# Fetching three attention weights already transposed by DMA, in place of turning them on TensorE, in a one-core recurrent-memory kernel

## The chip, the cores and the metric

The kernel runs on one core of one Trainium2 chip. The metric is the device time of one execution in microseconds (us). A separate execution, taken by the hardware profiler, gives the trace that is read here; its span is the time from the first to the last recorded instruction. PE is TensorE's matmul side and PEld its weight load, DVE is VectorE, ACT ScalarE, POOL GpSimd, SP the engine that issues most DMAs. L83 is line 83 of the kernel.

## The reference

Four layers follow one another on a bf16 tensor x of 2048 tokens by 448 features: attention with a recurrent memory, a gated feed-forward part, and both once more with the same weights. Cut to what matters:

```python
def attention(x, mem0, Wq, Wk, Wv, Wo, seg_len):        # 16 heads of 256, 8 memory rows
    mem = mem0
    for s in range(2048 // 32):
        h = concat([mem, x[32 * s:32 * s + 32]])        # 40 rows
        q, k, v = h @ Wq, h @ Wk, h @ Wv                # per head
        p = softmax(where(mask, q @ k.T * 256 ** -0.5, -1e9))
        o = (p @ v) summed over the heads through Wo
        mem = o[:8]                                     # feeds the next segment
        outs.append(o[8:])
x = x + attention(layernorm(x), ...)
x = x + (relu(n @ W_gate) * (n @ W_up)) @ W_down        # n = layernorm(x)
x = x + attention(layernorm(x), ...)
x = x + the same feed-forward part
```

Wq, Wk and Wv are 448 x 4096 each (16 heads of 256), Wo is 4096 x 448, all bf16: 3.67 MB each.

## The kernel before

The memory makes the 64 segments a chain. So the kernel does not form q, k and v per segment. It **fuses the weights first**: per head, A = Wq Wk^T (448 x 448) and B = Wv Wo (448 x 448), kept in SBUF as `A_sb` and `B_sb`. Then 69 steps (L747) follow, in which both attention layers run as two chains, the second `LAG` = 4 segments behind, and the feed-forward part of a block is fed in between (class `Feed`, L372).

The change touches only the fusing, L200 to L325, which comes ahead of the steps. TensorE contracts over the partitions of both operands, and A contracts over the head's 256 features, while Wq and Wk lie in memory with the 448 model features as rows. So each must be turned. The work goes in eight pairs of heads, p = 0 to 7, twice:

- **The q/k loop** (L272). `load_nat` (L215) brings 512 columns of a weight (two heads) in their natural layout into one of six tiles `nat` of 128 x 4 x 512: one DMA of 384 rows (L219, 384 KB), one of the last 64 rows (L220, 64 KB), and for Wq those 64 rows once more, into the other half of the partitions (L222). `flips` (L233) turns it: a `half` (L237) is eight 128 x 128 transposes on TensorE (`tr`, L85, tile `tpw`) and one copy of 128 x 1024 out of PSUM by DVE or ACT (L243). Two halves make one turned tile, `qT` or `kT`. Pair p's product is eight groups (kd, eo) of two matmuls of 384 columns (`aps`, L282) and two of 64 (`mxw`, L286), and copies into `A_sb` (L290 to L299).
- **The v loop** (L303). Pair p needs `vT`, turned likewise, and `wo`, 448 KB of Wo, fetched by POOL's queue (L308) into four buffers. Seven PSUM tiles `bps` of 448 columns are formed (L314 and L323) and copied into `B_sb`.

The turning is worked one pair ahead: `queue(p + 1)` (L247) gives the units of the next pair, and they are strewn between the groups of the present pair (L296, L317). TensorE's order is the program's order by hand: `in_order` (L74) chains every matmul and transpose to the one before. The other engines' instructions are ordered by the scheduler. `share` (L227) gives each copy out of PSUM to DVE or ACT, whichever has less by its table of costs. After p = 2 comes `first_rows` (L256): the normalised first 128 tokens are transposed on TensorE; their `rstd` is made on POOL (L161), behind POOL's memsets of L207 to L212.

PSUM tiles rotate through seven buffers. The tiles of the fusing lie in the pool `pre`, and the tiles of the steps (pool `main`, L334: `hk`, `Y1`, the feed-forward weights and others) are laid over it. The feed-forward weights come in pieces, each DMA tied to a point of TensorE's order (`next_piece`, L362).

Of the kernel before, what the change touches and what calls it, by code (L numbers as in the profile page):

```python
# [8 lines left out]
BF = mybir.dt.bfloat16  # L9
# [6 lines left out]
DM = 448  # L16
H = 16
NP = 8
# [36 lines left out]
def build_kernel(ctx, tc, A_x, A_mem0, A_Wq, A_Wk, A_Wv, A_Wo, B_W_gate, B_W_up, B_W_down, out,  # L55
                 ntiles=16, nseg=64):
    nc = tc.nc
    P = nc.NUM_PARTITIONS
# [4 lines left out]
    Wq = A_Wq.rearrange("d h e -> d (h e)")  # L63
    Wk = A_Wk.rearrange("d h e -> d (h e)")
    Wv = A_Wv.rearrange("d h e -> d (h e)")
# [3 lines left out]
    psum = ctx.enter_context(tc.tile_pool(name="psum", bufs=7, space=bass.MemoryType.PSUM))  # L69
# [4 lines left out]
    def in_order(r):  # L74
        if last_pe[0] is not None:
            tc.add_manual_dep(r.ins, last_pe[0],
                              mybir.DependencyInfo(mybir.DependencyClass.NoSync,
                                                   mybir.DependencyReason.DATA),
                              reason="order of issue")
        last_pe[0] = r.ins.name  # L80
# [4 lines left out]
    def tr(*a):  # L85
        in_order(nc.tensor.transpose(*a))  # L86
# [11 lines left out]
    def block(i):  # L98
        return slice(TB * i, TB * i + TB)
# [3 lines left out]
    ident = glob.tile([P, P], BF, name="ident")  # L103
# [19 lines left out]
    for b in range(4):  # L123
        o = 0 if b % 2 == 0 else MEM
# [8 lines left out]
    half = glob.tile([P, 1], F32, name="half")  # L133
# [6 lines left out]
    for i in range(2):  # L140
        t = glob.tile([P, BLK, HW], BF, name=f"hT{i}")
# [55 lines left out]
        nc.vector.tensor_copy(mem_of(g, cs)[:, 0:src.shape[1]], src)  # L197


    with tc.tile_pool(name="pre", bufs=6) as pre:  # L200
        mem0_n = pre.tile([MEM, 512], BF, name="mem0_n", bufs=1)
        nc.gpsimd.dma_start(mem0_n[:, 0:DM], mem0)
        nc.gpsimd.dma_start(mem0_n[:, DM:512], mem0[:, 384:DM])
        nats = []
        for i in range(6):
            t = pre.tile([P, 4, 512], BF, name=f"nat{i}", bufs=1)
            (nc.gpsimd if i % 2 else nc.vector).memset(t[64:128, 3, :], 0.0)  # L207
            nats.append(t)
        nc.gpsimd.memset(A_sb[64:128, 3, :, :, :], 0.0)
        nc.gpsimd.memset(A_sb[0:64, 3, 0, 0:4, :], 0.0)  # L210
        for t in TQ + TZ + PX + PM + YB:
            nc.gpsimd.memset(t[:], 0.0)  # L212
        nn = [0]

        def load_nat(src, p, eng):  # L215
            t = nats[nn[0] % 6]
            nn[0] += 1
            cols = slice(512 * p, 512 * (p + 1))
            eng.dma_start(t[:, 0:3, :], src[0:384, cols].rearrange("(k p) n -> p k n", p=P))  # L219
            eng.dma_start(t[0:64, 3, :], src[384:448, cols])  # L220
            if src is Wq:
                eng.dma_start(t[64:128, 3, :], src[384:448, cols])  # L222
            return t

        spent = {nc.vector: 0.0, nc.scalar: 0.0}

        def share(dst, src, n, per):  # L227
            cost = {nc.vector: 60 + n * per[0], nc.scalar: 170 + n * per[1]}
            eng = min(cost, key=lambda e: spent[e] + cost[e])
            spent[eng] += cost[eng]  # L230
            evac(eng, dst, src)

        def flips(src, p, name):  # L233
            nat = load_nat(src, p, nc.sync)
            o = pre.tile([P, 4, 512], BF, tag="tT", name=name)

            def half(e2):  # L237
                tp = psum.tile([P, 2, 512], BF, tag="ps", name="tpw")
                for e in range(2):
                    for kd in range(4):  # L240
                        tr(tp[:, e, kd * 128:(kd + 1) * 128],
                           nat[:, kd, (2 * e2 + e) * 128:(2 * e2 + e + 1) * 128], ident[:])
                share(o[:, 2 * e2:2 * e2 + 2, :], tp[:], 1024, (0.6, 0.82))  # L243

            return o, [lambda: half(0), lambda: half(1)]

        def queue(p):  # L247
            if p < NP:
                qT, a = flips(Wq, p, "qT")
                kT, b = flips(Wk, p, "kT")  # L250
                return (qT, kT), a + b
            if p == NP:
                return flips(Wv, 0, "vT")
            return None, []

        def first_rows():  # L256
            xn0 = normed(row_stats(xp[1]))
            if nblk > 3:
                nc.sync.dma_start(xp[1][0:TB, :], x_dram[block(3)])
            tps0 = transpose_tokens(xn0)  # L260
            for b in range(2):
                rows_in(nc.vector, b, 0, tps0[:, :, block(b)])
            mtp = psum.tile([P, 4, MEM], BF, tag="ps", name="mtp")
            for kd in range(4):
                tr(mtp[:, kd, :], mem0_n[:, kd * 128:(kd + 1) * 128], ident[0:MEM, 0:MEM])
            nc.vector.tensor_copy(mem0T[:], mtp[:])
            set_mem(0, mem0T[:].unsqueeze(2), (0,))

        ready, todo = queue(0)
        for u in todo:  # L270
            u()
        for p in range(NP):  # L272
            hf, p4 = divmod(p, 4)
            qT, kT = ready
            ready, todo = queue(p + 1)
            mx_ps = psum.tile([P, 4, 128], F32, tag="ps", name="mxw")
            for kd in range(4):
                for eo in range(2):
                    aps = psum.tile([P, 3, 128], F32, tag="ps", name="aps")
                    for t in range(2):  # L280
                        e = 2 * eo + t
                        mm(aps[:, :, :], qT[:, e, kd * 128:(kd + 1) * 128],  # L282
                           kT[:, e, 0:384], start=(t == 0), stop=(t == 1))
                    for t in range(2):
                        e = 2 * eo + t
                        mm(mx_ps[:, kd, eo * 64:eo * 64 + 64], qT[:, e, kd * 128:(kd + 1) * 128],  # L286
                           kT[:, e, 384:448], start=(t == 0), stop=(t == 1))
                    t0 = eo * 4 + p4
                    if kd < 3:
                        share(A_sb[:, kd, hf, t0:t0 + 17:8, :], aps[:], 384, (1.28, 0.85))  # L290
                    elif upper(hf, eo):
                        share(A_sb[64:128, 3, hf, t0, :], aps[64:128, 0, :], 128, (1.28, 0.85))
                        share(A_sb[0:64, 3, hf, t0 + 8:t0 + 17:8, :], aps[0:64, 1:3, :], 256, (1.28, 0.85))
                    else:
                        share(A_sb[0:64, 3, hf, t0:t0 + 17:8, :], aps[0:64], 384, (1.28, 0.85))
                    if todo and 2 * kd + eo in (0, 2, 4, 5):  # L296
                        todo.pop(0)()
            share(A_sb[:, 0:3, hf, 24 + p4, :], mx_ps[:, 0:3, :], 384, (1.28, 0.85))
            share(A_sb[0:64, 3, hf, 24 + p4, :], mx_ps[0:64, 3, :], 128, (1.28, 0.85))  # L299
            if p == 2:  # L300
                first_rows()

        for p in range(NP):  # L303
            hf, p4 = divmod(p, 4)
            vT = ready
            ready, todo = flips(Wv, p + 1, "vT") if p + 1 < NP else (None, [])
            wo = pre.tile([P, 4, DM], BF, tag="wo", name="wo", bufs=4)
            nc.gpsimd.dma_start(wo[:], Wo[:, 4 * p:4 * p + 4, :])  # L308
            for eo in range(2):
                for kd in range(3):  # L310
                    bps = psum.tile([P, 512], F32, tag="ps", name="bps")
                    for t in range(2):
                        e = 2 * eo + t
                        mm(bps[:, 0:DM], vT[:, e, kd * 128:(kd + 1) * 128], wo[:, e, :],  # L314
                           start=(t == 0), stop=(t == 1))
                    share(B_sb[:, hf, tidx(kd, eo, p4), 0:DM], bps[:, 0:DM], DM, (1.28, 0.85))
                    if kd == 1 and todo:  # L317
                        todo.pop(0)()
            bps = psum.tile([P, 512], F32, tag="ps", name="bps")
            for t in range(2):  # L320
                for eo in range(2):
                    e = 2 * eo + t
                    mm(bps[64 * eo:64 * eo + 64, 0:DM], vT[:, e, 384:448], wo[:, e, :],  # L323
                       start=(t == 0), stop=(t == 1), tile_position=(0, 64 * eo))
            share(B_sb[:, hf, 24 + p4, 0:DM], bps[:, 0:DM], DM, (1.28, 0.85))  # L325
# [12 lines left out]
    for i in range(2):  # L338
        t = main.tile([P, 5, 128], BF, name=f"hk{i}")
# [406 lines left out]
    pre = {}  # L746
    for g in range(nsteps + 1):  # L747
        if g == LAG - 1:
            set_mem(LAG, mem0T[:].unsqueeze(2), (1,))
        i = (g - 3) // 2  # L750
        pre = step(g, Feed(i) if g % 2 and 0 <= i < nblk + LAG // BLK - 1 else None, pre)
# [66 lines left out]
```

## Time and profile before

| what | value |
|---|---|
| three runs | 1678.39, 1678.39, 1681.45 us; median 1678.39 |
| the profiled execution's own time | 1679.21 us |
| its span | 1677.4 us (1.8 us lie around it) |
| granted TensorE clock, mean | 0.995 |
| PE busy over the span | 1630.9 us (97%), 41152 matmuls |
| DVE, ACT, POOL busy | 1184.3 (71%), 689.4 (41%), 87.8 us (5%) |
| HBM read | 23.70 MB |
| q/k loop, from its first product to the first `bps` | 9.0 to 47.5 us |
| v loop, to the first projection of the steps | 47.5 to 76.7 us |

Nearly the whole span is the 69 steps, with TensorE busy; the fusing is the first 76.7 us, 4.6% of it. Only that stretch holds the DMAs of Wq, Wk, Wv and Wo. Busy shares over the whole span say nothing of it, so it is read by stretches of its own.

### The profile page before, as it was taken

The numbers are of one execution on the slowest core, as the hardware profiler recorded it, in microseconds if no ns is written. First come the engines' busy times: TensorE is split into PE (matmuls) and PEld (weight loads), VectorE is DVE, ScalarE is ACT, GpSimd is POOL, SyncE is SP. The second block draws the span as 40 slices with busy tenths as digits, with TensorE's granted clock in tenths as the row PEclk, the third lists the DMA queues.
The fourth block names the chain that finished last, engine by engine and source line by source line (L and its number), as shares of the span: only waits on it lengthen the run. The fifth ranks groups of instructions, "written<-read, shape, count | busy, mean of one in ns | idle before, by whom it ended". The sixth has DMA issues, their size and how long they took to land.

```text
span 1677.4 us, 90576 instructions
## 1 busy us (share of the span) xinstructions
PE 1630.9 (97%) x41152; PEld 1523.0 (91%) x41152; DVE 1184.3 (71%) x4181; ACT 689.4 (41%) x2093; POOL 87.8 (5%) x178
## 2 busy tenths in 40 slices
PE   8999999999999999999999999999999999999997
PEld 6688999999999999999999999999999999999986
DVE  7766777777667767776677677766776777666774
ACT  6634443344333433443334334433344344333432
POOL 5200000000000000000000000000000000000000
PEclk9989999999999999999999999999999999999999
DMA  9430000000000000000000000000000000000000
GB/s 271 127 91 14 8 9 9 8 5 9 9 9 9 9 9 8 4 9 9 9 9 9 9 9 5 8 9 9 9 9 9 9 6 7 9 8 6 6 7 5
DMA packets 26785, 33.17 MB, mean 20 GB/s; under 512 B 3352, under 2 KB 24736, under 8 KB 26400
## 3 DMA queue, kind: packets, MB, share of 16 engines
q1 hardware_dynamic: 25312, 23.70, 5.0%
q8 instruction: 322, 5.28, 1.3%
q0 software_dynamic: 1088, 3.68, 0.7%
q14 instruction: 63, 0.52, 0.1%
HBM read 23.70 MB, written 1.84 MB: 15 GB/s over the span
## 4 chain that ended last, share of the span: by engine, by line
PE 84%; DVE 11%; ACT 2%; issue 1%; DMA 0%; POOL 0%; POOLq 0%; SPq 0%; DVEq 0%; ACTq 0%
PE prj L83 31%; PE ox L83 16%; PE ups L83 6%; PE gps L83 6%; PE dps L83 5%; PE o L83 5%; PE y L83 3%; PE Sx L83 2%; DVE Y L92 2%; DVE ssum L503 1%; PE bps L83 1%; PE tpw L86 1%; PE tps L86 1%; DVE mx L499 1%; PE aps L83 1%
## 5 line engine op out<-in xcount | busy, mean ns | idle before, releaser
L83 PE MATMUL prj<-hT,A_sb 128*128 128x80 bf16 (+3 forms) x15232 | 570.2, 199 | 1.0 <-issue 0.5
L83 PEld LDWEIGHTS <-A_sb 128*128 128x128 bf16 (+1 forms) x15232 | 544.0, 99 | 5.7 <-issue 1.6
L83 PEld LDWEIGHTS <-B_sb 128*128 128x128 bf16 (+1 forms) x15232 | 491.0, 103 | 17.5 <-issue 0.2
L83 PE MATMUL ox<-Y,B_sb 128*128 128x80 bf16 (+4 forms) x11424 | 438.7, 199 | 0.0
L90 ACT CAST TQ<-prj 128x320 bf16<-128x320 f32 (+1 forms) x456 | 170.0, 385 | 160.5 <-PE prj L83 128.2
L92 DVE CAST TQ<-prj 128x320 bf16<-128x320 f32 (+1 forms) x456 | 192.9, 430 | 44.6 <-PE prj L83 38.4
L90 ACT CAST Y<-y 128x512 bf16<-128x512 f32 (+2 forms) x384 | 145.7, 417 | 84.1 <-DVE Y L92 72.1
L92 DVE CAST Y<-y 128x128 bf16<-128x128 f32 (+2 forms) x384 | 161.4, 458 | 18.5 <-PE y L83 3.6
L83 PE MATMUL ups<-xT,Wu_sb 128*128 128x128 bf16 (+1 forms) x1904 | 140.6, 217 | 1.3 <-DVE xT L395 0.5
L83 PE MATMUL gps<-xT,Wg_sb 128*128 128x128 bf16 (+1 forms) x1904 | 140.5, 217 | 0.0
L83 PEld LDWEIGHTS <-hk 40*128 40x128 bf16 (+1 forms) x1950 | 102.2, 95 | 25.1 <-issue 10.9
L501 ACT ACTIVATE se<-se 128x80 f32<-128x80 f32 (+1 forms) x270 | 80.1, 303 | 102.2 <-DVE se L500 100.6
L635 ACT COPY os<-o 64x80 f32<-64x80 f32 (+3 forms) x68 | 14.9, 219 | 250.2 <-PE o L83 249.0
L408 ACT CAST ut<-ups 128x256 bf16<-128x256 f32 (+1 forms) x238 | 84.5, 355 | 69.5 <-PE ups L83 48.5
L83 PEld LDWEIGHTS <-Wg_sb 128*128 128x128 bf16 x1904 | 112.4, 99 | 0.7 <-issue 0.6
L409 DVE SCALAR_TENSOR_TENSOR hh<-gps,ut 128x256 bf16<-128x256 f32 (+1 forms) x238 | 93.1, 401 | 26.6 <-PE gps L83 15.3
L83 PEld LDWEIGHTS <-Wu_sb 128*128 128x128 bf16 x1904 | 110.7, 99 | 1.0 <-issue 1.0
L83 PE MATMUL dps<-Wd_sb,hh 128*128 128x448 bf16 x476 | 95.7, 353 | 0.0
L161 POOL TENSOR_SCALAR rstd<-mv 128x1 f32<-128x1 f32 x67 | 14.9, 223 | 1525.9 <-DVE mv L159 1476.4
L642 DVE TENSOR_TENSOR hT<-o,os 64x16 bf16<-64x16 f32 (+1 forms) x134 | 22.8, 170 | 98.3 <-ACT os L639 58.9
L418 DVE TENSOR_TENSOR xp<-dps,xa 64x448 bf16<-64x448 f32 x32 | 20.1, 627 | 95.2 <-PE dps L83 95.2
L90 ACT CAST TZ<-prj 64x320 bf16<-64x320 f32 (+2 forms) x152 | 56.1, 379 | 71.9 <-DVE TZ L92 68.8
(120 smaller groups left out, 2069.2 us busy)
## 6 DMA issues: line engine op xcount, KB each, us to landing
wo<-in_A_Wo_dram POOLq DMA_DIRECT2D x8, 448.0 KB, 5.4
nat<-in_A_Wq_dram SPq DMA_DIRECT2D x8, 384.0 KB, 5.5
nat<-in_A_Wk_dram SPq DMA_DIRECT2D x8, 384.0 KB, 4.9
nat<-in_A_Wv_dram SPq DMA_DIRECT2D x8, 384.0 KB, 4.6
xa<-in_A_x_dram SPq DMA_DIRECT2D x32, 56.0 KB, 2.2
xa<-xp SPq DMA_DIRECT2D x32, 56.0 KB, 1.9
out_dram<-xa SPq DMA_DIRECT2D x32, 56.0 KB, 2.0
xp<-in_A_x_dram SPq DMA_DIRECT2D x30, 56.0 KB, 2.1
```

Source lines behind the costliest of these rows:

```text
L83: in_order(nc.tensor.matmul(*a, **k))
L86: in_order(nc.tensor.transpose(*a))
L90: nc.scalar.copy(dst, src)
L92: eng.tensor_copy(dst, src)
L161: nc.gpsimd.tensor_scalar(out=rstd[:], in0=mv[:, 1:2], scalar1=EPS, scalar2=None, op0=ALU.add)
L408: nc.scalar.copy(ut[:, :, n], ups[:, :, n])
L409: nc.vector.scalar_tensor_tensor(out=hh[:, 2 * u:2 * u + 2, n], in0=gps[:, :, n], scalar=0.0, in1=ut[:, :, n], op0=ALU.max, op1=ALU.mult)
L418: nc.vector.tensor_tensor(self.nx[TB:P, :], dps[TB:P, 0:DM], self.x[TB:P, :], op=ALU.add)
L499: nc.vector.tensor_reduce(mx[:], Sp[:], axis=AX.X, op=ALU.max)
L501: nc.scalar.activation(se[:], se[:], AF.Exp, scale=SCALE)
L503: nc.vector.tensor_reduce(ssum[:], se[:], axis=AX.X, op=ALU.add)
L642: nc.vector.tensor_tensor(mem_of(g + 1, ms)[r, 3], o3[r, m0:m0 + nm].rearrange("p (c m) -> p c m", m=MEM), os[r, m0:m0 + nm].rearrange("p ...
```

## The change

Wq, Wk and Wv are no longer loaded in their natural layout. `flipped_in` asks the DMA to write 448 rows x 512 columns transposed: column n goes to partition n mod 128 of chunk n div 128, the rows lie beside one another. For Wq a second transposing DMA writes the last 64 rows once more behind them (columns 448 to 512 of the tile). The natural tiles, their memsets, the TensorE transposes and the copies out of PSUM go. Three pairs of qT and kT are asked for ahead of the loop, then pair p + 3 at the start of pair p; from p = 5 on, two tiles of vT in place of a pair. The pool `pre` has 12 turned tiles in place of 6 (and six natural ones less: the same space).

```diff
-    with tc.tile_pool(name="pre", bufs=6) as pre:
+    with tc.tile_pool(name="pre", bufs=12) as pre:
...
-        nats = []
-        for i in range(6):
-            t = pre.tile([P, 4, 512], BF, name=f"nat{i}", bufs=1)
-            (nc.gpsimd if i % 2 else nc.vector).memset(t[64:128, 3, :], 0.0)
-            nats.append(t)
...
-        def flips(src, p, name):
-            nat = load_nat(src, p, nc.sync)
+        def flipped_in(src, p, name):
             o = pre.tile([P, 4, 512], BF, tag="tT", name=name)
-
-            def half(e2):
-                tp = psum.tile([P, 2, 512], BF, tag="ps", name="tpw")
-                for e in range(2):
-                    for kd in range(4):
-                        tr(tp[:, e, kd * 128:(kd + 1) * 128],
-                           nat[:, kd, (2 * e2 + e) * 128:(2 * e2 + e + 1) * 128], ident[:])
-                share(o[:, 2 * e2:2 * e2 + 2, :], tp[:], 1024, (0.6, 0.82))
...
+            nc.sync.dma_start_transpose(o[:, :, 0:DM], src[:, 512 * p:512 * (p + 1)])
+            if src is Wq:
+                nc.sync.dma_start_transpose(o[:, :, DM:512], src[384:DM, 512 * p:512 * (p + 1)])
+            return o
...
-        ready, todo = queue(0)
-        for u in todo:
-            u()
+        turned = [(flipped_in(Wq, p, "qT"), flipped_in(Wk, p, "kT")) for p in range(3)]
         for p in range(NP):
             hf, p4 = divmod(p, 4)
-            qT, kT = ready
-            ready, todo = queue(p + 1)
+            qT, kT = turned.pop(0)
+            if p + 3 < NP:
+                turned.append((flipped_in(Wq, p + 3, "qT"), flipped_in(Wk, p + 3, "kT")))
+            else:
+                turned += [flipped_in(Wv, 2 * (p + 3 - NP) + i, "vT") for i in range(2)]
...
-                    if todo and 2 * kd + eo in (0, 2, 4, 5):
-                        todo.pop(0)()
...
-            vT = ready
-            ready, todo = flips(Wv, p + 1, "vT") if p + 1 < NP else (None, [])
+            vT = turned.pop(0)
+            if p + 6 < NP:
+                turned.append(flipped_in(Wv, p + 6, "vT"))
...
-                    if kd == 1 and todo:
-                        todo.pop(0)()
```

On the queues: SP issues 32 transposing DMAs (16 for Wq, 8 for Wk, 8 for Wv) where it issued 56 loads. The first eight DMAs of SP go out with no wait but for SP itself, from then on each waits for the one eight before it; the transposing ones of pair 6 and later wait for TensorE to be done with the tile twelve before. The reload of `xp` (L259 before), which waits for DVE's normalised rows, stands between the last two DMAs of Wq, and the loads of `xa` stand behind all of Wv.

More of the change, by code (lines that the diff above doesn't have):

```diff
@@ L212, in build_kernel @@
             nc.gpsimd.memset(t[:], 0.0)
[L213 to L223, printed above, removed]
         spent = {nc.vector: 0.0, nc.scalar: 0.0}
@@ L231, in share @@
             evac(eng, dst, src)
-        def flips(src, p, name):
-            nat = load_nat(src, p, nc.sync)
+        def flipped_in(src, p, name):
             o = pre.tile([P, 4, 512], BF, tag="tT", name=name)
-            def half(e2):
-                tp = psum.tile([P, 2, 512], BF, tag="ps", name="tpw")
-                for e in range(2):
-                    for kd in range(4):
-                        tr(tp[:, e, kd * 128:(kd + 1) * 128],
-                           nat[:, kd, (2 * e2 + e) * 128:(2 * e2 + e + 1) * 128], ident[:])
-                share(o[:, 2 * e2:2 * e2 + 2, :], tp[:], 1024, (0.6, 0.82))
[L245 to L254, printed above, removed]
+            nc.sync.dma_start_transpose(o[:, :, 0:DM], src[:, 512 * p:512 * (p + 1)])
+            if src is Wq:
+                nc.sync.dma_start_transpose(o[:, :, DM:512], src[384:DM, 512 * p:512 * (p + 1)])
+            return o
         def first_rows():
```

## The prediction

> **What bounds the kernel now.** I read the page's engine totals first (PE 97% of the span), then the busy time by stretch around the code that changes, then that stretch's instructions by form, the chain that ended last, and the DMA queues by window. The stretches, with busy us (count) of PE, PEld, DVE, ACT, POOL, then granted clock, DMA share and GB/s:
>
> ```profile
> 5.30:9.00 3.70, 3.40 (x32) 2.89 (x33) 1.44 (x3) 1.26 (x2) 3.70 (x3) 1.00 0.93 285
> 9.00:24.10 15.10, 15.08 (x201) 11.84 (x201) 12.58 (x24) 10.96 (x23) 15.02 (x18) 1.00 1.08 299
> 24.10:47.60 23.50, 23.50 (x307) 18.27 (x306) 18.83 (x38) 17.34 (x35) 0.90 (x3) 1.00 0.93 279
> 47.60:76.70 29.10, 29.10 (x241) 16.00 (x238) 21.21 (x34) 20.03 (x39) 8.12 (x9) 1.00 0.32 95
> ```
>
> PE has no gap from 9 to 76.7 us, at clock 1.00: the fusing is bound by TensorE. But the DMA engines are full beside it until about 47 us, at 279 to 299 GB/s: the second limit stands close behind the first. The chain of waits says the same: it starts with one DMA wait and then is PE alone, a piece of it eight transposes long:
>
> ```profile
> 1.18 4.09 DMA nat<-in_A_Wq_dram
> 5.31 2.94 PE tpw L86 x24
> 8.27 0.70 DVE kT L92
> 9.02 0.48 PE aps L83 x2
> ...
> 48.38 0.45 PE tpw L86 x8
> 48.83 1.14 PE bps L83 x6
> ```
>
> **What goes.** By form, in the first 140 us (count, busy, mean ns):
>
> ```profile
> L86 PE MATMUL tpw<-ident,nat 128*128 128x128 bf16 x384 | 30.3, 225 | 5.3 <-DMA nat<-in_A_Wq_dram 5.3
> L92 DVE COPY vT<-tpw 128x1024 bf16<-128x1024 bf16 x14 | 9.7, 689 | 2.6 <-PE tpw L86 2.6
> L90 ACT COPY qT<-tpw 128x1024 bf16<-128x1024 bf16 x5 | 5.1, 1012 | 6.6 <-PE tpw L86 6.5
> ```
>
> The 384 transposes are 48 halves of eight; a half holds the chain for 0.45 us (the mean of 225 ns overlaps), 48 x 0.445 = 21.4 us. Four halves lie ahead of the first product, 30 in the q/k loop, 14 in the v loop. So, without them, q/k costs PE 38.4 - 13.4 = 25.0 us (3.1 a pair; the timeline shows 0.38 per group of four matmuls, x8), and v 29.1 - 6.3 = 22.8 us (2.85 a pair). The 48 copies, 37 on DVE and 11 on ACT (0.69 and 1.01 us each), lay beside PE, so they are no gain of their own. The copies that stay still fit: per q/k pair eight of about 0.52 us and two smaller, 4.9 us over two engines, against 3.1 us of PE. The memsets of `nat` go as well: 1.5 us of POOL's queue, ahead of the memsets that precede `rstd`.
>
> **What comes: the rate of a transposing DMA.** The trace has none, and everything hangs on it. Bytes: 3 x 3.67 MB and the second 64 rows of Wq, 0.52 MB: 11.53 MB transposed, plus Wo, 3.67 MB plain, half of it beside the q/k loop (four buffers).
>
> One end is the plain rate, 299 GB/s. For the other I price small pieces by the DMA queues of three windows (10 to 20, 78 to 90 and 300 to 400 us): packets, MB, share of 16 engines.
>
> ```profile
> q1 hardware_dynamic: 3154, 2.99, 108.8%
> ...
> q1 hardware_dynamic: 451, 1.44, 39.6%
> ...
> q1 hardware_dynamic: 640, 0.46, 1.8%
> ```
>
> The third is 28.8 engine-us, mostly rows of 896 B, the second 76.0, rows of 3584 B. A line through both is 9.4 ns a packet plus 0.050 ns a byte; it gives 178 engine-us for the first, which shows 174. There the queue ran at 1.09 of 16 engines, so I multiply by 1.09. How small are the pieces here? Column n of a source row goes to partition n mod 128, so a piece of a row that fills one chunk is 128 elements, 256 B: 22 ns, **202 GB/s** for 16 engines. Along a destination partition the run follows the source rows; 448 and 64 rows have blocks of 64 or of 16 in common, 128 B or 32 B: **141** and **51 GB/s**. All of these are estimates from those rows. Single elements I exclude: it is an instruction of its own kind (the changed program's SP order shows it), with no call for 2-byte pieces.
>
> The end E of the fusing (76.7 us before) is then the later of two paths. By DMA: 3.3 us to the first byte landed (issue at 1.2 plus the 2.1 us of `xp`), the transposed bytes at rate R, Wo's 12.2 us at 300 GB/s on the same engines, and the last pair's 2.85 us. By PE: 3.3 us, the q/k bytes (7.86 MB at R, Wo's half 6.1), the last q/k pair 3.1, then 22.8 us of v.
>
> - R = 299: 61.5 us by PE, a gain of 15.2.
> - R = 202: 75.4 by DMA, 74.2 by PE: a gain of 1.3.
> - R = 141: 3.3 + 81.8 + 12.2 + 2.85 = 100.1, a loss of 23.4.
> - R = 100: 133.6, a loss of 57. R = 51: 244, a loss of 168.
>
> It breaks even at 198 GB/s. I take 141: between ends as far apart as 299 and 51 the nearest rows are those of small pieces, and a transposing write is short on both sides, so the 256 B read alone is a best case. **The sum is 1679.2 + 23.4 = 1702.6 us** against the profiled execution's own 1679.21 (span 1677.4 and 1.8 around it). That time is 0.8 us above the median, so the loss against the median is 24.2, or 1.4%.
>
> The Trainium skill speaks against the change on the page "VectorE: DVE Perf Modes" (The three transpose paths): a 128 x 128 bf16 transpose is 390 ns on TensorE and 1309 ns by DMA. TensorE's row here is 219 ns alone, 56 in a stream of eight; no run here shows the other. One at a time, the 368 blocks (estimate) would take 482 us, a kernel near 2.1 ms.
>
> **Other edits.** SP: 56 loads at 0.37 to 0.59 us each (longer where they wait) become 32; a transposing one may hold SP longer, and decides only from about 2.3 us each ((73.8 - 1.2) / 32); I add nothing, since eight may be in flight. Behind a waiting SP stand `xa` and the feed-forward weights, used 50 us later in the steps: hidden. The `xp` reload waits for DVE's rows, ready about 20 us (POOL's `rstd` chain ended at 21.5 us, less 1.5); at 141 GB/s SP reaches it about 38 us, no cost; at 299 about 20, just even. `first_rows` is TensorE's new wait if DMA is fast: pair 2 could end at 16.2 us and would stand until 20.5. That is swallowed: from 20.5, five pairs end at 36.0, and the DMA path already says 38.7. At 141 pair 2 lands at 24 us, so no wait.
>
> **The rivals.**
> 1. **Faster: the transpose runs near the plain rate.** Place: the q/k loop; it decides from 198 GB/s up. For it: plain DMAs ran at 299 in rows of only 1 KB, and a DMA that reshapes many rows at once need not pay per piece. Against: the loop already has its engines full, and the fit falls with size. From 215 to 299 GB/s: 73.4 to 61.5 us, 1676 to **1664 us**. The Trainium skill, "Advanced Engine Details and Errata" (X-Bar Transpose (TRN2)), says it outright: transposing DMAs are as fast as regular ones; "DMA: Bandwidth & Descriptors" (Latency and other measured facts) has 261 GB/s where the rows are not contiguous, as here. By 261 the sum would be 65.4 us, or 1668 (estimate). Chance 0.34.
> 2. **A draw**, 185 to 213 GB/s, the price of 256 B pieces: 1676 to 1683 us, about **1678**. Chance 0.11.
> 3. **Far slower: pieces of 32 B, or blocks moved one by one**: under 100 GB/s, from 1736 to **1847 us** (51 GB/s). For it: 16 is the block that any row count here shares. Against: the share would have to be nearly all per-packet cost. Chance 0.17.
> That the transposes stay on TensorE is excluded: the changed program's PE order has no `tpw`.
>
> **How the numbers follow.** Forecast: 100 to 185 GB/s, 1683 to 1736 us, chance 0.38. Range for 8 in 10: rivals 1 and 2 and the forecast, 0.83, so 1664 to 1736; the likeliest case's own range is 1683 to 1736. A measurement of this kernel tells about 0.2% (3.4 us) from no change. Faster by more is rival 1, 0.34; within it rival 2, 0.11; slower 0.38 + 0.17 = 0.55.
>
> **What would show it.** In the profile after: no `tpw`; the first projection at about 100 us, everything behind it as before but later; PE in 9 to 90 us with gaps put down to DMAs of `qT`, `kT`, `vT`, about half busy; DMA share still near 1 but at some 140 GB/s beside Wo; copies on DVE and ACT of 0.48 to 0.62 us as now. Rival 1 shows pairs 3.3 to 3.8 us apart and projections from 62 to 73 us; rival 3 pairs 10 us or more apart. The forecast is wrong if the transfers keep above 198 GB/s, or if SP, not the engines, sets their pace.

## The result and the profile after

The changed kernel takes 1686.52 us (median of 15 runs, 1679.77 to 1690.83), the kernel before 1679.45 beside it (15 runs, 1677.58 to 1681.45). The ratio is 1.0037, interval 1.0025 to 1.0049 (worked out from all runs, so it is not quite the ratio of the two medians, here and below): slower by 0.4%. The forecast had the sign, but 1702.6 us; of its loss of 23.4 us some 7 were there.

The profiled execution took 1686.52 us too, with a span of 1684.7 against 1677.4: 7.3 us more. The first projection, the end E of the fusing, is at 84.55 us against 76.7: 7.8 us more. So the whole loss lies ahead of the steps, and only that stretch needs reading. From the page of the changed kernel, the engine totals and the DMA queues (packets, MB, share of 16 engines):

```profile
PE 1616.9 (96%) x40768; PEld 1503.9 (89%) x40768; DVE 1172.8 (70%) x4152; ACT 674.3 (40%) x2071; POOL 86.3 (5%) x175
...
DMA packets 60702, 33.13 MB, mean 20 GB/s; under 512 B 48536, under 2 KB 58656, under 8 KB 60320
...
HBM read 12.17 MB, written 1.84 MB: 8 GB/s over the span
```

PE has the 384 transposes less (41152 to 40768) and 14.0 us less to do, and the kernel is slower all the same. Nearly 48,500 packets are now under 512 B: the 11.53 MB transposed, cut into 256 B, are 45,000. (The count of HBM reads fell from 23.70 to 12.17 MB, by just the transposed bytes, though the same weights are read: it seems to leave the transposing reads out.)

The stretches, with the columns of the prediction's first fence: two pieces of the q/k loop, then the q/k loop and the v loop as wholes.

```profile
10.00:20.00 10.00, 4.65 (x33) 2.63 (x32) 9.95 (x12) 1.90 (x4) 9.92 (x15) 0.78 0.93 199
40.00:50.00 10.00, 8.62 (x74) 5.26 (x73) 5.28 (x11) 4.87 (x12) 0.00 (x0) 0.85 0.98 202
8.20:56.80 48.60, 32.01 (x264) 19.34 (x264) 28.16 (x53) 17.75 (x42) 15.24 (x20) 0.86 1.02 196
56.80:84.50 27.70, 24.86 (x132) 10.41 (x131) 16.51 (x28) 16.09 (x31) 9.82 (x10) 0.94 1.08 180
```

Before, PE was busy without a gap at clock 1.00 while the DMA engines moved 279 to 299 GB/s. Now the DMA engines are full (share near 1) at about 200 GB/s, and PE waits for them: 32 of 48.6 us busy. Even that is flattered, since the granted clock fell to 0.78 to 0.87 there and a pair of `aps` matmuls often took 0.64 us in place of 0.33. The v loop takes 27.7 us where the sum had 22.8 of PE; PE was busy for 24.9 of them, at a clock of 0.94.

The chain that ended last, from 18 us on (start, us, what):

```profile
18.67 1.83 SPq L218
20.55 5.21 SPq L218
25.81 3.76 SPq L220
29.61 8.26 DMA kT<-in_A_Wk_dram
38.00 0.80 PE aps L83 x2
...
56.99 10.59 PE bps L83 x59
67.58 11.11 DMA vT<-in_A_Wv_dram
78.73 5.82 PE bps L83 x32
84.55 2.90 PE prj L83 x112
```

Two places stand out. Up to 20 us SP holds each transposing DMA 1.5 to 1.9 us (L218; 1.25 us for the 64 rows, L220), and pairs come 4.6 to 5.1 us apart. At 20.5 us two holds grow to 5.2 and 3.8 us and the `kT` after them takes 8.3 from issue to landing; at 67.6 us a vT tile takes 11.1 us. Both are where POOL's queue fetches Wo. The DMA queues in a stretch without Wo (40 to 50 us), and in the first with it (20 to 36 us; q0 is POOL's queue, q1 SP's):

```profile
q1 hardware_dynamic: 7810, 2.00, 96.5%
```

```profile
q0 software_dynamic: 512, 1.84, 55.8%
q1 hardware_dynamic: 4379, 1.10, 55.8%
```

Without Wo: 0.965 x 16 x 10 us / 7810 = 19.8 ns per 256 B, 202 GB/s. Beside Wo: 32.6 ns per 256 B and 279 ns per packet of Wo (4480 and 1792 B, 3584 on average). The two together moved 184 GB/s. At 202 and 300 GB/s they would have needed 5.5 + 6.1 = 11.6 of the 16 us. In the kernel before, the same four loads of Wo stand on POOL's queue in the same window, 20 to 36 us, but beside plain loads:

```profile
q1 hardware_dynamic: 3160, 2.91, 66.2%
q0 software_dynamic: 512, 1.84, 35.8%
```

There a packet of Wo took 179 ns, and the two queues together moved 299 GB/s. So POOL's queue is not slow beside any other stream, but beside the transposing one. The single packets in the trace say how: the median packet of 256 B took 18 ns with Wo and without, but beside Wo 5% of them took over 100 ns, and these hold 45% of the stream's packet time (0.5% and 8% without Wo). Most pass as before, and a few stand long.

The 202 GB/s are an average too. The GB/s in quarter-microsecond slices, 10 to 20 us:

```profile
GB/s 54 131 227 84 211 283 293 287 294 89 211 272 284 293 279 265 191 54 160 72 0 58 164 285 292 288 291 291 198 49 156 137 58 187 289 290 291 282 256 72
```

For about a microsecond at a time the transposing stream moves near 290 GB/s, as plain loads did, and then it falls far below 200 for as long.

### The profile page after: what moved, and what is told of

The parts are those of the page before. It is cut to its first block, busy times and chain, and to the rows that moved or that the text cites. A ratio compares the mean times of both kernels' runs of the same rounds, so it can differ in the third digit from the quotient of the medians.

```text
span 1684.7 us, 89682 instructions
## 1 busy us (share of the span) xinstructions
PE 1616.9 (96%) x40768; PEld 1503.9 (89%) x40768; DVE 1172.8 (70%) x4152; ACT 674.3 (40%) x2071; POOL 86.3 (5%) x175
## 3 DMA queue, kind: packets, MB, share of 16 engines
q1 hardware_dynamic: 59232, 23.70, 6.6%
HBM read 12.17 MB, written 1.84 MB: 8 GB/s over the span
## 4 chain that ended last, share of the span: by engine, by line
PE 82%; DVE 11%; ACT 2%; SPq 2%; DMA 1%; issue 1%; POOL 0%; POOLq 0%; ACTq 0%
PE prj L83 31%; PE ox L83 16%; PE ups L83 6%; PE gps L83 6%; PE dps L83 5%; PE o L83 5%; PE y L83 3%; PE Sx L83 2%; DVE Y L92 2%; DVE ssum L468 1%; PE tps L86 1%; DVE mx L464 1%; SPq L218 1%; PE ya L83 1%; ACT se L466 1%
## 5 line engine op out<-in xcount | busy, mean ns | idle before, releaser
L607 DVE TENSOR_TENSOR hT<-o,os 64x16 bf16<-64x16 f32 (+1 forms) x134 | 22.8, 170 | 97.9 <-ACT os L604 59.8
L83 PE MATMUL y<-PT,hk 40*128 40x256 bf16 (+1 forms) x1280 | 84.2, 251 | 1.1 <-DVE PT L480 1.1
```

Source lines behind the costliest of these rows:

```text
L83: in_order(nc.tensor.matmul(*a, **k))
L607: nc.vector.tensor_tensor(mem_of(g + 1, ms)[r, 3], o3[r, m0:m0 + nm].rearrange("p (c m) -> p c m", m=MEM), os[r, m0:m0 + nm].rearrange("p ...
```

## The experiments

Three theories were tested. **D**: the time of the DMA engines decides, the transposed bytes at about 200 GB/s and Wo beside them. **S**: SP decides, because it is held by each transposing DMA, so their number counts. **W**: Wo's loads on POOL's queue beside the transposing stream cost more than their bytes. Ratios are against the kernel before, run beside each; E is the first projection in the profile.

**1. Wq's second DMA dropped.** The last 64 rows of Wq are used once only, by products of 64 rows put to the right half of the array.

```diff
-            if src is Wq:
-                nc.sync.dma_start_transpose(o[:, :, DM:512], src[384:DM, 512 * p:512 * (p + 1)])
...
+                        if kd == 3 and upper(hf, eo):
+                            mm(aps[64:128, 0, :], qT[:, e, 384:448], kT[:, e, 0:128],
+                               start=(t == 0), stop=(t == 1), tile_position=(0, 64))
```

> The second transposing DMA of Wq (64 rows) is dropped for all eight pairs; the products that read it use 64 weight columns, and the one that must land in partitions 64 to 127 is placed there on TensorE. Theory S (SP's hold of every transposing DMA sets the pace: 1.25 us for 64 rows, 1.5 to 1.9 us for 448, measured in the changed kernel's trace): a pair costs SP 3.4 us in place of 4.75, the steps start 8 to 11 us earlier than in the changed kernel (84.6 us), at 74 to 77 us, about 1677 us. Theory D (the step of the prediction: the DMA engines' price per 256 B piece, 202 GB/s, sets the pace): only the bytes go, 0.52 MB, 2.6 us, so 82 us and about 1684. Theory W (the stretches beside Wo decide): within 2 us of the changed kernel unless a 64-row DMA lies in such a stretch, then 2.5 to 4 us.

1683.21 us, ratio 1.0034 (1.0012 to 1.0055): not told from the change. E is 82.83, 1.7 us earlier. Eight of 32 issues are gone, and SP gets through the bytes no faster; its chain:

```profile
2.85 2.03 SPq L218
...
4.92 2.10 SPq L218
...
7.06 2.40 SPq L218
...
9.50 2.07 SPq L218
```

The remaining holds grew from 1.5 to 1.9 us to 2.0 to 2.4, and the engines moved the same 199 GB/s between 10 and 20 us. So the hold is back-pressure: SP is let go as fast as the engines take bytes. S falls by this. The 0.52 MB saved are worth 2.6 us at 202 GB/s; the 1.7 us of E agree with that but do not show it, since E differs by more between profiles of kernels that are alike (experiment 6).

**2. Wo left out.** Wo's eight loads are not made and a constant tile stands in for them, so the output is not the reference's.

```diff
+        wo = pre.tile([P, 4, DM], BF, name="wo", bufs=1)
+        nc.vector.memset(wo[:], 0.01)
...
-            nc.gpsimd.dma_start(wo[:], Wo[:, 4 * p:4 * p + 4, :])
```

> Wo's eight loads are left out (one tile filled with a constant stands in for them, so the B products are of that constant). Theory W (sharing with Wo's queue costs the transposing stream more than Wo's bytes): the three issues that held SP 5.2, 3.8 and 6.1 us fall back to 1.25 to 1.9, 10 us, and the 11 us wait for vT goes; the steps start at 69 to 72 us, about 1672. The prediction's plain sum by bytes takes 12.2 us off for Wo: 72.4 us, 1674. Theory S alone, Wo being hidden: within 3 us of the changed kernel. In the first 20 us nothing changes under any of them: 4.6 to 4.9 us a pair.

1675.16 us, ratio 0.9973 (0.9961 to 0.9985); E 71.73, 12.8 us earlier. Up to 25 us the q/k pairs still come 4.6 to 5.3 us apart (198 GB/s between 10 and 20 us), but the v loop is now PE alone, without a gap, for 22.9 us. Wo's presence costs the changed kernel 12.8 us, more than all that it lost. This cannot say how much of that is bytes (12.2 us at 300 GB/s) and how much is more: W's 69 to 72 and the 72.4 of a plain sum by bytes both fit.

**3. Only Wv transposed by DMA.** The kernel before, with Wv's tiles asked for four ahead and Wq and Wk turned on TensorE.

```diff
-            vT = ready
-            ready, todo = flips(Wv, p + 1, "vT") if p + 1 < NP else (None, [])
+            vT = turned.pop(0)
+            if p + 4 < NP:
+                turned.append(flipped_in(Wv, p + 4, "vT"))
```

> Wq and Wk are loaded and turned as in the kernel before; only Wv comes by transposing DMA, four tiles ahead. TensorE loses 16 of 48 halves of eight transposes (0.445 us each), 7.1 us; eight transposing DMAs hold SP some 14 us and lie beside the q/k loop's second half and the v loop. If the gain of the removed TensorE work is real where the transfers have room: the steps start at 69.6 us, about 1672 to 1673, 0.4% faster than before. If Wo's last four loads stall vT as in the changed kernel: 73 to 77 us, 1676 to 1680.

1678.11 us, ratio 0.9984 (0.9972 to 0.9996); E 76.34. In the kernel before, the DMA engines were mostly idle in the v loop (share 0.32), and still taking the 6.3 us of transposes out of it bought almost nothing. The share is now 0.96, at 158 GB/s. The chain of this kernel shows what took them:

```profile
59.92 13.36 DMA wo<-in_A_Wo_dram
73.28 0.14 issue
73.41 2.93 PE bps L83 x16
76.34 2.90 PE prj L83 x112
```

A Wo tile that took 5.4 us from issue to landing in the kernel before (median) takes 13.4 us beside transposing DMAs, and TensorE waits for it. This fits theory W.

**4. Transposing DMAs of 1024 columns**, two pairs each, in half as many tiles.

```diff
-            o = pre.tile([P, 4, 512], BF, tag="tT", name=name)
-            nc.sync.dma_start_transpose(o[:, :, 0:DM], src[:, 512 * p:512 * (p + 1)])
+            o = pre.tile([P, 8, 512], BF, tag="tT", name=name)
+            cols = slice(1024 * p, 1024 * (p + 1))
+            nc.sync.dma_start_transpose(o[:, :, 0:DM], src[:, cols])
```

> As the changed kernel, but each transposing DMA brings 1024 columns (two pairs of heads), so 16 in place of 32 of them, the same bytes in the same 256 B pieces. Theory S with a fixed hold (about 1.2 us each plus 0.5 us per 459 KB): SP needs 3.6 us a pair in place of 4.75; the steps start 6 to 10 us earlier, 75 to 79 us, about 1679, though the first product starts 3 to 4 us later. Theory D: the pace is unchanged, the later first product costs 3 to 4 us, 87 to 89 us, about 1690. If the hold grows with the tiles instead of being fixed: as theory D.

1684.84 us, ratio 1.0038 (1.0021 to 1.0054); E 81.30. The hold doubled with the bytes, 3.5 to 3.9 us for 448 x 1024 away from Wo: again not S. The rate rose a little, to 219 to 228 GB/s, but beside Wo one hold was 11.58 us and a landing 13.55, and the time stayed that of the change. E lies between what S (75 to 79) and D (87 to 89) were expected to give. That fewer and wider DMAs moved the same packets about a tenth faster says that the price goes in part by the DMA, not by the packet alone.

**5. Wo on SP's own queue**, in line: vT, Wo, vT, Wo, from pair 4 of the q/k loop on, with eight Wo buffers and eleven turned tiles.

```diff
+            if p >= 4:
+                for i in (2 * p - 8, 2 * p - 7):
+                    vT = flipped_in(Wv, i, "vT")
+                    wo = pre.tile([P, 4, DM], BF, tag="wo", name="wo", bufs=8)
+                    r = nc.sync.dma_start(wo[:], Wo[:, 4 * i:4 * i + 4, :])
+                    turned.append((vT, wo))
...
-            nc.gpsimd.dma_start(wo[:], Wo[:, 4 * p:4 * p + 4, :])
```

> As the changed kernel, but Wo comes on SP's own queue in line with the transposing DMAs (vT, Wo, vT, Wo, ... behind the last kT; eight Wo buffers, 11 turned tiles in place of 12), not on POOL's queue beside them. In the changed kernel the two stretches beside Wo took some 4.5 us more each than transposed bytes at 200 GB/s plus Wo's bytes at 300. Theory W (two queues that take turns packet by packet cost more than their bytes): the excess goes; first v product at 45 to 47 us, steps from 75 to 77 us, about 1678. Rival (transposing and plain traffic mix badly on the same engines whatever the queue): the excess stays, 82 to 85 us, about 1685.

1679.06 us, ratio 1.0003 (0.9994 to 1.0012): a draw; E 76.95, 7.6 us earlier than with the change. Its DMA queue from 44 to 72 us, where most of Wo comes:

```profile
q1 hardware_dynamic: 18881, 7.06, 114.0%
```

By the sizes of the packets in the trace that is 3.80 MB transposed and 3.25 plain. At 202 and 300 GB/s they would take 18.8 + 10.8 = 29.6 us; it took 28. In line, the two prices simply add. They do not in the changed kernel.

**6. One pair ahead**, in place of three, with the same order on SP.

```diff
-        turned = [(flipped_in(Wq, p, "qT"), flipped_in(Wk, p, "kT")) for p in range(3)]
+        turned = [(flipped_in(Wq, p, "qT"), flipped_in(Wk, p, "kT")) for p in range(1)]
```

> As the changed kernel, but one pair is asked for ahead of its use, not three. SP's queue has the same instructions in the same order with the same waits, and SP is held by the transfers and not by the loop, so every theory that puts the pace in the DMA engines expects no difference: steps from 83 to 86 us, within 0.2% of the changed kernel. Rival (the depth of asking is what keeps TensorE fed): 3 us or more later per pair that is not covered, 1690 us and over.

1687.39 us, ratio 1.0045 (1.0031 to 1.0060): not told from the change. The profile's E, 88.85, is 3 us outside what was expected; its holds beside Wo were 5.5 and 10.4 us. Between the profiles of the change, of this kernel and of experiment 7, E differs by up to 4.3 us, and the difference lies in the stretches beside Wo. The depth written in the program makes no difference: SP issues as fast as the engines let it, and the tiles, not the loop, limit how far it runs.

**7. DVE's masks first.** In the changed kernel TensorE once waits 5.3 us for a copy of DVE, which had the four small instructions for the masks in front of it (last section). Here the scheduler is made to put them ahead of the first copy.

```diff
+            if masks_done:
+                tc.add_manual_dep(r.ins, masks_done.pop(),
```

> As the changed kernel, but DVE does the eleven small mask instructions ahead of its first copy of a product, as in the kernel before; in the changed kernel they came behind it, fell among POOL's memsets, four of them took 7.75 us in place of 1.1, and TensorE stood 5.35 us for the copy queued behind them. If the DMA path sets the end, this wait was covered: the masks take about 1.1 us at 4 us, the 5.35 us go, and the steps still start at 83 to 86 us. If it was on the path: 79 to 81 us, about 1682.

1687.08 us, ratio 1.0043 (1.0026 to 1.0059); E 88.28, where 83 to 86 was expected. The 5.3 us wait is gone and the end is no earlier: it was covered by the transfers, which are the later path there (holds of 11.64, 2.83 and 4.84 us beside Wo).

**8. Only Wv transposed, Wo fetched ahead of it.** Experiment 3 with seven Wo buffers: four loads on POOL's queue as before, three on SP's ahead of the first vT, the last in line.

```diff
+        for p in range(7):
+            fetch_wo(p, nc.gpsimd if p < 4 else nc.sync)
         turned = [flipped_in(Wv, p, "vT") for p in range(4)]
```

> Only Wv by transposing DMA, as in the run before of that kind (steps from 76.3 us, where the last Wo loads took 13 us to land beside the transposes); now Wo has seven buffers, its loads 4 to 6 stand on SP's queue ahead of the first transposing DMA and the last one in line with them. If mixing Wo into the transposing stretch was what ate the gain: TensorE sets the end again, steps from 69.5 to 72 us, 1672 to 1674.5, 0.3 to 0.4% faster than before. If not: 75 us and over, 1678.

1674.42 us (1672.49 to 1676.08), ratio 0.9971 (0.9961 to 0.9981): 0.3% faster than the kernel before, and the fastest of all that were run. E 70.85. Its q/k loop and v loop:

```profile
9.00:47.90 38.90, 38.90 (x491) 29.94 (x489) 30.72 (x60) 27.67 (x56) 21.10 (x25) 1.00 1.08 276
47.90:70.80 22.90, 22.90 (x131) 9.77 (x128) 16.40 (x27) 15.86 (x32) 0.00 (x0) 1.00 0.67 133
```

PE has no gap in either, at full clock. In the v loop the transposes on PE are gone (22.9 us, where it was 29.1), and the transposing DMAs have room: share 0.67. Fetching Wo earlier cannot have been the gain by itself, since PE had no gap to fill in the kernel before.

**9 and 10. Experiment 5 with Wo on POOL's queue, and on ACT's.** The same tiles and buffers; each Wo load is tied to the product ahead of it, so that it is beside the transposing DMAs. Experiment 10 has the same edit with `nc.scalar`.

```diff
-                    r = nc.sync.dma_start(wo[:], Wo[:, 4 * i:4 * i + 4, :])
+                    r = nc.gpsimd.dma_start(wo[:], Wo[:, 4 * i:4 * i + 4, :])
+                    tc.add_manual_dep(r.ins, last_pe[0],
```

> As the run with Wo on SP's queue (eight Wo buffers, 11 turned tiles), but Wo's loads go on POOL's queue, two at the end of each of the pairs 4 to 7 of the q/k loop, so beside the transposing DMAs again. Theory W (two queues side by side cost more than their bytes, wherever Wo stands): the stretches beside Wo run at 185 GB/s or less in total, steps from 81 to 86 us, 1683 to 1688. Rival (the gain of the SP run came from the buffers and the later place, not from the one queue): 75 to 78 us, about 1679.

> As that run, but Wo's loads are issued by ScalarE's queue at the same points. If any second queue beside the transposing one costs the excess: steps from 81 to 86 us, as with POOL. If it is POOL's queue in particular (its packets are 3.4 KB, one behind another on each engine): 75 to 79 us. ScalarE's copies stand behind its waits for a free DMA slot, which may add 1 to 3 us to either.

On POOL's queue: 1689.19 us, ratio 1.0058 (1.0041 to 1.0075); E 90.38, 13.4 us later than in experiment 5. On ACT's: 1693.13 us, ratio 1.0083 (1.0068 to 1.0098); E 90.99. The DMA queues from 40 to 60 us, first with POOL's (q0), then with ACT's (q10):

```profile
q0 software_dynamic: 743, 2.64, 62.8%
q1 hardware_dynamic: 2550, 0.67, 48.3%
```

```profile
q1 hardware_dynamic: 10373, 2.64, 85.0%
q10 hardware_dynamic: 1720, 1.50, 31.0%
```

Beside POOL's queue SP's gets 0.67 MB through in 20 us (0.61 of them transposed), at 60.6 ns a packet; PE does nothing from 50 to 60 us. By the prices, what passed needed 3.3 + 8.8 = 12.1 us. 18% of the 256 B packets took over 100 ns there. So W stands for POOL's queue. The 13.4 us of E are not all of this kind: on a queue of their own, six of Wo's eight loads go out by 44.3 us, beside the last `kT` (issued at 40.2, landed at 61.2 us), which the q/k loop needs sooner; in experiment 5 they stand behind it. This may be why E is later than the 81 to 86 expected.

Beside ACT's queue the stream kept 2.64 MB, and by the prices what passed needed 13.1 + 5.0 = 18.1 of the 20 us: here the two about add. That kernel's time, outside both its expected ranges, tells nothing of the queue, since the copies that ACT has to make stood behind its DMA issues, which wait (its chain runs over ACT's queue and copies). But by the rates this second queue, with two loads at a time on it, did not starve the stream. What it is in POOL's queue that does so stays open: its loads differ from those of SP and ACT in the kind of queue and also in the size of packet, 4480 and 1792 B against 896, and no run separates the two.

## Why the prediction came out so

- **What goes: right.** 384 transposes and 48 copies went, the copies cost no time, and the v loop without transposes is 22.9 us of PE where it has its data (experiments 2 and 8), against 22.8 worked out.
- **That the DMA engines become the bound: right.** Share near 1, PE waiting for `qT`, `kT`, `vT`.
- **"I take 141": the step that failed.** I let the shorter runs of the destination set the price, 128 B, and called the 256 B read "a best case". The trace shows 256 B packets, 19.8 ns each, 199 to 206 GB/s where Wo is not beside them. So the term of 81.8 us was 57.1, 24.7 too much, and by my own sign ("wrong if the transfers keep above 198 GB/s") the forecast was wrong. My line through the plain rows had 202 for 256 B, but that it met the rate is partly luck: the line prices every packet alike, and the trace has stretches near 290 GB/s with gaps around them, and up to 228 with DMAs twice as wide.
- **"Wo's 12.2 us at 300 GB/s on the same engines": the second step that failed, too small.** I added Wo's bytes as if two streams shared the engines at their own prices. With 57.1 us in the sum E would be 75.4, rival 2, a draw; it is 84.55. By window, time over the price of the bytes moved (202 and 300 GB/s): 0.4 us from 5 to 20, **4.4** from 20 to 36, 0.3 from 36 to 57, **2.5** from 57 to 79. These 7.6 us lie beside Wo, but for 0.7, and 7.6 us is what experiment 5 wins by putting Wo in line. The last wait for vT also leaves two pairs behind it, 5.8 us, not the 2.85 of one; that is 3.0 more. 75.4 + 7.6 + 3.0 = 86.0; the start was about 1 us better than its term.
- So the sign was right by luck as much as by reason: two errors of unlike size, 24.7 too much and 9.1 too little, leave 15.6 us, the distance of the forecast. **"It breaks even at 198 GB/s"** holds for experiment 5, which runs at 202 and draws. It does not hold for the change, which runs at 202 and loses.
- **SP, "I add nothing": right**, and for the reason that experiments 1 and 4 show: the hold, away from Wo 1.5 to 2.2 us and so under the 2.3 us named, follows the engines.
- **`first_rows` and the `xp` reload, hidden: right**; no wait for them is on the chain. (The reload's issue holds SP for 0.59 us on it.)
- **Rival 1** stood on the rule of the Trainium skill, "Advanced Engine Details and Errata" (X-Bar Transpose (TRN2)), that a transposing DMA is as fast as a regular one. This trace does not agree: 202 GB/s where the plain loads of the kernel before ran at 299 between 9 and 24 us. I gave that rule 0.34.
- **Not foreseen:** DVE's masks (covered), and the wider spread of the times, 11 us against 4. Experiments 6 and 7 suggest the stretch beside Wo as its source; that was not tried by itself.

## What to carry to other kernels

Price a transposing DMA by a rate measured for its shape (202 GB/s here, with packets of 256 B), not by its destination's runs, and ask first whether the DMA engines have room: in the q/k loop they had none, so taking 15 us of work off TensorE there only moved the bound; in the v loop they had, and the same edit was worth 0.3% once Wo was out of its way. Do not run a transposing stream beside plain loads of POOL's queue: fetch those ahead, or put them in line on the same queue (experiments 3, 5, 8 and 9). How many tiles the program asks for ahead says little when the issuing queue runs by itself until the engines push back.

## What the runs showed of the hardware

- Two DMA streams need not add by bytes: transposing and POOL's plain loads together moved 167 GB/s (experiment 9, 40 to 60 us), 184 and 208 (the change, 20 to 36 and 57 to 79 us); transposing and plain loads in line on SP's queue 253; plain loads of both queues 299 (the kernel before, 20 to 36 us).
- SP is held by a transposing DMA, and the longer the slower the engines take its bytes: 1.5 to 2.4 us for 448 x 512, 3.5 to 3.9 for 448 x 1024, beside Wo up to 11.6 (experiments 4 and 7) and 16.5 us (experiment 9). It is not in proportion to the bytes: 64 x 512 took 1.25.
- With PE idle a third of the q/k loop, the granted clock of what it did fell too, to 0.78 to 0.87 (windows of 10 us from 10 to 50 us, where before it was 1.00).
- Four mask instructions of DVE, 32 columns wide, were held while POOL wrote its memsets. DVE's groups up to 30 us, in the changed kernel, and then in experiment 7, where they run before the memsets (count, busy us, mean ns):

```profile
L125 DVE TENSOR_SCALAR maskS<-keyf,rowf 128x32 bf16<-128x32 f32 x4 | 7.7, 7489 | 0.0
```

```profile
L92 DVE CAST A_sb<-aps 128x384 bf16<-128x384 f32 x9 | 5.0, 556 | 9.5 <-PE aps L83 9.5
...
L130 DVE TENSOR_SCALAR maskS<-keyf,rowf 128x32 bf16<-128x32 f32 x4 | 0.7, 240 | 0.0
```

  240 ns became 7.5 us, until the memsets ended at 18.3 us; copies out of PSUM beside the same memsets kept 556 ns. The Trainium skill, "SBUF — State Buffer" (Who interferes with whom), says that POOL and a DVE instruction of this kind (`tensor_scalar`) can block each other through a shared pair of ports. The trace agrees, and shows a block that outlasts one instruction of POOL: the longest memset in those 7.5 us took 1.95 us.
